# Block attention and expert mixture: first two chunks in plain float32, first block's loads in halves

## The chip, the cores and the metric

One core of a Trainium2 chip. The metric is the device time of one execution in microseconds; lower is better.

## The reference, cut to what matters

q, k, v are 4 × 8 × 576 × 64 float32. Attention is causal by blocks of 64 tokens; its output, laid out as x [2304, 512], goes into a mixture of four experts.

```python
scores = scale * np.matmul(q, k.transpose(0, 1, 3, 2))
mask = (pos[:, None] // 64) >= (pos[None, :] // 64)
attn = softmax(np.where(mask, scores, -1e9))
x = np.matmul(attn, v)                      # as [2304, 512]
p = domain_probs / (domain_probs.sum(-1, keepdims=True) + 1e-9)
for e in range(4):
    h = np.maximum(x @ w1[e], 0.0)          # 512 -> 1024
    out += p[:, e:e + 1] * (h @ w2[e])      # 1024 -> 512
```

## The kernel before, in words

The tokens are cut into a first block of 256 (the first 64 of each of the four batches) and four blocks of 512. The mixture runs through 160 chunks: block by block, expert by expert, eight slices of 128 hidden columns each. A chunk has a first product (`mm1`, L961), a relu and a second product (`mm2`, L1006), which adds into the accumulators of the block's 128-token tiles (two tiles for the first block, four for the others).

Matrix products keep float32 accuracy in split form: an operand is cast to the narrower fp32r type (the high part: xh, w1h, w2h, hh) and the rest is subtracted out (the low part: xl, w1l, w2l, hl), and a product is the sum of three fp32r matmuls. So the first product of a chunk is 12 matmuls (4 slices of the 512 inputs, 3 terms) and the second 3 for each tile. Weights are cast on ACT or DVE (L326, `a_copy`) and subtracted on DVE (L333, `tt`) in `w_split`; the relu is an ACT operation into hh (L978) and a DVE operation into hl (L980).

The attention of the first block (`first_block`, L787 to 903) has no mask and runs in four steps, each for two batches and half of the head pairs: transposes of k and q on PE (L821), copies, scores (L841), then max, subtraction, exp, sum, reciprocal and product (L856 to L866, DVE but for the exp on ACT), transposes (L870), probabilities times V (L883), and the split of the result into xh (ACT) and xl (DVE). PE fills its gaps until the first `mm1` with matmuls on a constant (L345, `warm_up`, 512 columns); WARM = 9 of them stand at the start.

The attention of the other blocks runs in units (one batch, two heads) beside the mixture. A unit transposes k and q on DVE (kT L398, qT L432), has its scores on PE (L510 for the first units, in plain float32), their evacuation on ACT and DVE (tiles S and cm), a column maximum over all partitions on POOL (L644, `m_thread`), a subtraction on DVE, exp on ACT (L660, 128 × 1536 each), and probabilities times V on PE (L723).

The order is made when the kernel is built. Every sequence of operations is a generator; class `Flow` keeps a clock for each engine, and `run` always issues the operation that can start first by its estimate of costs, and among those that can start by then the one with the lowest priority number. It also emits the fill matmuls, as many as its estimate of PE's gap holds. So a changed cost or priority moves instructions on every engine, and what is written behind a waiting instruction on the same engine waits as well. Nearly all loads go out on the SP queue (`dma`, L320); the first block's q and half of its v go out on ACT's. Chunk weights are loaded by `w_thread` (256 KB for each of w1 and w2 of a chunk) into two raw buffers each.

## Time and profile before

| what | value |
|---|---|
| median of 3 runs (lowest, highest) | 935.22 us (934.63, 935.36) |
| profiled execution | 934.92 us |
| its span, instructions | 933.1 us, 12703 |
| PE busy | 922.1 us, 99% of the span |
| weight loads of PE (beside matmuls) | 759.0 us |
| DVE, ACT, POOL busy | 727.8, 424.2, 140.6 us |
| granted clock of PE | 0.999 of full |
| moved by DMA | 107.83 MB, mean 116 GB/s |

The profile is one execution. Busy time of an engine is the union of its instructions; a timeline row gives the start and the duration of one instruction or of several like ones, and in brackets how long the engine stood idle before it and what released it. Matmuls are pipelined: the distance between two starts, not the duration, is what one costs. A matmul in plain float32 leaves two records.

### The profile page before, as it was taken

The numbers are of one execution on the slowest core, as the hardware profiler recorded it, in microseconds if no ns is written. First come the engines' busy times: TensorE is split into PE (matmuls) and PEld (weight loads), VectorE is DVE, ScalarE is ACT, GpSimd is POOL, SyncE is SP. The second block draws the span as 40 slices with busy tenths as digits, with TensorE's granted clock in tenths as the row PEclk, the third lists the DMA queues.
The fourth block names the chain that finished last, engine by engine and source line by source line (L and its number), as shares of the span: only waits on it lengthen the run. The fifth ranks groups of instructions, "written<-read, shape, count | busy, mean of one in ns | idle before, by whom it ended". The sixth has DMA issues, their size and how long they took to land.

```text
span 933.1 us, 12703 instructions
## 1 busy us (share of the span) xinstructions
PE 922.1 (99%) x4381; PEld 759.0 (81%) x4382; DVE 727.8 (78%) x1323; ACT 424.2 (45%) x726; POOL 140.6 (15%) x59
## 2 busy tenths in 40 slices
PE   8999999999999999999999999999999999999998
PEld 4777787888888888888888888888888888888886
DVE  6888879788998988878998889898987754545442
ACT  3477656645565445436454545454434322222220
POOL 2101100131212121212122202112121200000000
PEclk9999999999999999999999999999999999999999
DMA  9765447625352355452523546343523343333311
GB/s 167 169 172 149 125 144 177 160 69 138 89 133 77 102 131 152 97 128 79 142 69 99 127 125 161 100 107 113 116 84 88 99 148 98 95 101 92 100 57 45
DMA packets 235648, 107.83 MB, mean 116 GB/s; under 512 B 130880, under 2 KB 212800, under 8 KB 235584
## 3 DMA queue, kind: packets, MB, share of 16 engines
q1 hardware_dynamic: 232416, 106.24, 43.0%
q10 hardware_dynamic: 3168, 0.79, 0.5%
q8 instruction: 34, 0.56, 0.3%
q14 instruction: 30, 0.25, 0.1%
HBM read 102.27 MB, written 4.72 MB: 115 GB/s over the span
## 4 chain that ended last, share of the span: by engine, by line
PE 94%; DVE 2%; DMA 2%; ACT 1%; SPq 1%; issue 1%; DVEq 0%; ACTq 0%
PE h L961 42%; PE acc L1006 41%; PE att L723 5%; PE att L523 2%; PE att L522 2%; PE acc L723 1%; SPq L320 1%; DMA S<-in_k_dram 0%; DMA w2r<-in_moe_w_dram 0%; PE att L510 0%; DVE cm L333 0%; DMA kr<-in_k_dram 0%; DMA w1r<-in_moe_w_dram 0%; DVE o L1035 0%; PE acc L510 0%
## 5 line engine op out<-in xcount | busy, mean ns | idle before, releaser
L961 PE MATMUL h<-xh,w1h 128*128 128x512 f32 (+1 forms) x640 | 239.1, 374 | 0.6 <-ACT w1h L326 0.6
L961 PE MATMUL h<-xh,w1l 128*128 128x512 f32 (+1 forms) x640 | 236.1, 369 | 1.4 <-DVE w1l L333 1.4
L961 PE MATMUL h<-xl,w1h 128*128 128x512 f32 (+1 forms) x640 | 235.7, 368 | 0.0
L1006 PE MATMUL acc<-w2h,hh 128*128 128x512 f32 x576 | 226.3, 393 | 0.0
L1006 PE MATMUL acc<-w2l,hh 128*128 128x512 f32 x576 | 224.8, 390 | 0.0
L1006 PE MATMUL acc<-w2h,hl 128*128 128x512 f32 x576 | 224.5, 390 | 0.0
L978 ACT ACTIVATE hh<-h 128x512 fp32r<-128x512 f32 (+1 forms) x160 | 88.9, 556 | 206.9 <-PE h L961 204.1
L326 ACT CAST w2h<-w2r 128x512 fp32r<-128x512 f32 x153 | 95.1, 621 | 151.7 <-PE acc L1006 149.1
L333 DVE TENSOR_TENSOR w2l<-w2r,w2h 128x512 fp32r<-128x512 f32 x160 | 109.8, 686 | 53.3 <-ACT w2h L326 52.9
L961 PEld LDWEIGHTS h<-xh,w1h 128*128 128x128 f32 x640 | 120.7, 189 | 22.9 <-issue 2.2
L961 PEld LDWEIGHTS h<-xh,w1l 128*128 128x128 f32 x640 | 120.5, 188 | 22.3 <-DVE w1l L333 2.0
L961 PEld LDWEIGHTS h<-xl,w1h 128*128 128x128 f32 x640 | 120.7, 189 | 19.5 <-DVE xl L333 0.2
L980 DVE SCALAR_TENSOR_TENSOR hl<-h,hh 128x512 fp32r<-128x512 f32 (+1 forms) x160 | 100.8, 630 | 36.4 <-ACT hh L978 35.4
L1006 PEld LDWEIGHTS acc<-w2h,hl 128*128 128x128 f32 x576 | 108.2, 188 | 22.9
L1006 PEld LDWEIGHTS acc<-w2h,hh 128*128 128x128 f32 x576 | 108.3, 188 | 21.2 <-ACT w2h L326 0.7
L1006 PEld LDWEIGHTS acc<-w2l,hh 128*128 128x128 f32 x576 | 108.4, 188 | 20.1
L333 DVE TENSOR_TENSOR w1l<-w1r,w1h 128x512 fp32r<-128x512 f32 x160 | 114.4, 715 | 9.6 <-ACT w1h L326 5.9
L680 POOL PARTITION_ALL_REDUCE S<-S x24 | 81.3, 3437 | 240.2 <-DVE S L333 174.0
L644 POOL PARTITION_ALL_REDUCE mx<-cm x16 | 54.5, 3407 | 358.5 <-DVE cm L333 279.3
L326 ACT CAST w1h<-w1r 128x512 fp32r<-128x512 f32 x115 | 71.2, 619 | 16.7 <-DMA w1r<-in_moe_w_dram 16.4
L326 ACT COPY S<-att 128x512 f32<-128x512 f32 (+2 forms) x88 | 47.5, 540 | 54.5 <-DVE att L589 31.9
L333 DVE TENSOR_TENSOR S<-S,mx 128x1024 f32<-128x1024 f32 (+4 forms) x80 | 60.3, 791 | 4.0 <-POOL mx L644 4.0
(130 smaller groups left out, 855.5 us busy)
## 6 DMA issues: line engine op xcount, KB each, us to landing
w1r<-in_moe_w_dram SPq DMA_DIRECT2D x160, 256.0 KB, 2.9
w2r<-in_moe_w_dram SPq DMA_DIRECT2D x160, 256.0 KB, 2.8
qr<-in_q_dram SPq DMA_DIRECT2D x112, 64.0 KB, 2.3
kr<-in_k_dram SPq DMA_DIRECT2D x64, 72.0 KB, 2.9
out_dram<-o SPq DMA_DIRECT2D x16, 256.0 KB, 2.4
vr<-in_v_dram SPq DMA_DIRECT2D x24, 128.0 KB, 2.6
VN<-in_v_dram SPq DMA_DIRECT2D x8, 128.0 KB, 2.8
S<-in_k_dram SPq DMA_DIRECT2D x4, 128.0 KB, 4.6
```

The source lines that it names most:

```text
L320: o = op(q, 550.0, lambda e: (nc.sync if e == "sp" else nc.scalar).dma_start(out=dst, in_=src), r, u, prio)
L326: o = op(engs, 0, lambda e: nc.scalar.copy(dst, src) if e == "act" else nc.vector.tensor_copy(dst, src), r, u, prio)
L333: o = op(engs, 0, lambda e: ENG[e].tensor_tensor(out=dst, in0=a, in1=b, op=alu), r, u, prio)
L522: nc.tensor.matmul(out=o, lhsT=KK.tile[:, at:at + n], rhs=Hv[:, hs, lo:W], start=True, stop=False)
L523: nc.tensor.matmul(out=o, lhsT=KK.tile[:, at:at + n], rhs=Lv[:, hs, lo:W], start=False, stop=True)
L644: lambda _: nc.gpsimd.partition_all_reduce(mx.tile[:, :2 * W], src, P, RED.max),
L680: st["sums"].append((yield op("pool", 150 + 6.3 * W, lambda _, h=h: nc.gpsimd.partition_all_reduce(Sv[:, h, W:2 * W], Sv[:, h, :W], P, RED ...
L723: nc.tensor.matmul(out=o, lhsT=lhsT, rhs=rhs, start=(i == 0), stop=(i == n - 1))
L961: nc.tensor.matmul(out=ps[:, :n], lhsT=s.tile[:, ks], rhs=x.tile[:, kc, :n], start=(kc == 0 and m == 0), stop=(kc == KC - 1 and m == 2),)
L978: a = yield op("act", 0.833 * n + 55, lambda _: nc.scalar.activation(hh.tile[:, :n], ps[:, :n], AF.Relu), [mm], [pb, hh], 0.0)
L980: l = yield op("dve", 1.04 * n + 70, lambda _: nc.vector.scalar_tensor_tensor(out=hl.tile[:, :n], in0=ps[:, :n], scalar=0.0, in1=hh.tile[: ...
L1006: nc.tensor.matmul(out=acc, lhsT=s.tile[:, ts], rhs=w.tile, start=(f == 0 and m == 0), stop=(f == FC - 1 and m == 2))
```

## The change

- The first block's k and q loads are cut: the first step's halves of k and q go first (k on SP, q on ACT), the other halves of batches 0 and 1 later, on SP (`ORDER`). Chunk 0's w1 is issued on SP, too.
- Chunks 0 and 1 (`WHOLE = 2`) use x, w1, h and w2 as they are, in plain float32 matmuls (`whole1`: four of 256 columns; `whole2`: one of 512 for each tile). There are no splits of their weights, and their relu is one ACT operation (`relu0`). Their weights lie in buffers of the attention that are not used yet. x of the first block is kept whole (x0), and its split into xh and xl is made from that copy by `parts`.
- The costs of the first block's chain are changed by `near` (a lag of −180 ns, 80 ns more for each operation off PE); fill matmuls have 256 columns instead of 512 (the nine first ones keep 512), with a new formula for their number; casts of the weights of chunks 2 to 4 get a lag of 1000 ns; the units' maximum on POOL waits until the mixture is behind chunk 2.

What the order of SP's queue becomes at the start. Before (S1 are k and v of the first block, w1r0 and w2r0 the raw weights of chunk 0, kr, qr, VN the units' k, q and v):

```order
L320 DMA S1_112<-in_k_dram 64x8x64 x4
L320 DMA S1_112<-in_v_dram 64x8x64 x2
L320 DMA w1r0_77<-in_moe_w1_dram 128x4x128
L320 DMA w2r0_79<-in_moe_w2_dram 128x512
L320 DMA kr0_93<-in_k_dram 32x18x32 x4
L320 DMA qr0_95<-in_q_dram 32x16x32 x4
L320 DMA VN0_107<-in_v_dram 64x64
L320 DMA VN0_107<-in_v_dram 128x4x64
```

Now (vr0 is chunk 0's w1, tr0 its w2, qr0 and qT0 with in_moe are chunk 1's weights, w1r and w2r those of chunks 2 and 3):

```order
L342 DMA vr0_96<-in_moe_w1_dram 128x4x128
L342 DMA S1_112<-in_k_dram 64x4x64 x2
L342 DMA S1_112<-in_k_dram 64x8x64 x2
L342 DMA S1_112<-in_v_dram 64x8x64
L342 DMA S1_112<-in_k_dram 64x4x64 x2
L342 DMA cm0_117<-in_q_dram 64x4x64 x2
L342 DMA S1_112<-in_v_dram 64x8x64 x2
L342 DMA tr0_109<-in_moe_w2_dram 128x512
L342 DMA kr0_93<-in_k_dram 32x18x32 x4
L342 DMA qr0_95<-in_q_dram 32x16x32 x4
L342 DMA VN0_107<-in_v_dram 64x64
L342 DMA VN0_107<-in_v_dram 128x4x64
```

Chunk 0's w1 stands ahead of all of k, and its w2 behind k, q and v; the loads of chunks 1 to 3 follow in one row of six behind VN.

SP's queue around the load of chunk 6's w1 (w1r0 in the last row of each piece). Before:

```order
L320 DMA w1r1_78<-in_moe_w1_dram 128x4x128
L320 DMA w2r1_80<-in_moe_w2_dram 128x512
L320 DMA kr1_94<-in_k_dram 32x18x32 x2
L320 DMA qr0_95<-in_q_dram 32x16x32 x4
L320 DMA kr1_94<-in_k_dram 32x18x32 x2
L320 DMA w1r0_77<-in_moe_w1_dram 128x4x128
```

Now:

```order
L342 DMA w2r0_79<-in_moe_w2_dram 128x512
L342 DMA w2r1_80<-in_moe_w2_dram 128x512
L342 DMA kr1_94<-in_k_dram 32x18x32 x2
L342 DMA qr0_95<-in_q_dram 32x16x32 x4
L342 DMA kr1_94<-in_k_dram 32x18x32 x2
L342 DMA probs_n_134<-in_moe_domain_probs_dram 128x4 x4
L342 DMA w1r0_77<-in_moe_w1_dram 128x4x128
```

Four small loads of probs_n that stood ahead of chunk 4's w1 (two rows further up) now stand right ahead of chunk 6's w1. Counted from the start of the queue, 62 loads stood ahead of chunk 6's w1, and now 67.

ACT around the exps of unit 0 (S0, 128x1536). Before (hh1 in the second row shown is chunk 5's relu, w1h2 and w2h2 are chunk 6's casts):

```order
L326 CAST w1h2_63<-w1r0_77 128x512
L978 ACTIVATE hh1_82<-h1_122 128x256
L326 CAST w2h2_71<-w2r0_79 128x512
L660 ACTIVATE S0_111<-S0_111 128x1536
L978 ACTIVATE hh0_81<-h0_121 128x256
L326 CAST w1h3_64<-w1r1_78 128x512
L326 CAST w2h3_72<-w2r1_80 128x512
L660 ACTIVATE S0_111<-S0_111 128x1536
L326 CAST w1h0_61<-w1r0_77 128x512
```

Now (w1h0 and w2h0 are chunk 6's casts, hh1 in the sixth row chunk 5's relu):

```order
L1051 ACTIVATE hh0_81<-h0_121 128x256
L348 CAST w1h0_61<-w1r0_77 128x512
L682 ACTIVATE S0_111<-S0_111 128x1536
L348 CAST w2h0_69<-w2r0_79 128x512
L682 ACTIVATE S0_111<-S0_111 128x1536
L1051 ACTIVATE hh1_82<-h1_122 128x256
L348 CAST w2h1_70<-w2r1_80 128x512
L348 COPY S1_112<-att0_127 128x448
```

Chunk 5's relu stood ahead of both exps and of the cast of chunk 6's w2; now it stands behind them.

The diff, cut to its core:

```diff
-ORDER = [("k", 0), ("q", 0), ("k", 1), ("q", 1), ("v", 0), ("v", 1)]
+ORDER = [("k", 0, 0, 2, "ss"), ("q", 0, 0, 2, "aa"), ("k", 1, 0, 4, "ss"), ("q", 1, 0, 4, "aa"), ("v", 0, 0, 4, "sa"),
+         ("k", 0, 2, 4, "ss"), ("q", 0, 2, 4, "ss"), ("v", 1, 0, 4, "ss")]
 STEPS = [(0, 0, 2), (1, 0, 2), (0, 2, 4), (1, 2, 4)]
+WHOLE = 2
...
             if eng == "pe" and self.fill:
-                n = int(self.FILL * (t - self.clock["pe"]) / 216.0)
+                gap = t - self.clock["pe"]
+                n = int(self.FILL * (gap + 180.0) / 110.0) if gap > 0.0 else 0
...
+    x0 = fl.free["mx"][0].tile.rearrange("p (c w) -> p c w", c=KC)
+    h0s = [fl.free["rc"][0].tile[:, 256 * i:256 * i + 256] for i in range(WHOLE)]
+    wraw = [(fl.free["vr"][0].tile.rearrange("p t h d -> p (t h d)"), fl.free["tr"][0].tile),
+            (fl.free["qr"][0].tile[:, MAXW:], fl.free["qT"][0].tile[:, MAXW:])]
...
+    def near(o):
+        if isinstance(o.eng, list):
+            o.eng = [(e, c + 80.0) for e, c in o.eng]
+        elif o.eng != "pe":
+            o.cost += 80.0
+        o.lag = -180.0
+        return o
...
-            yield ("until", lambda: "S ready" in st)
+            yield ("until", lambda: "S ready" in st and now[0] > WHOLE)
...
+            for name, g, c0, c1, qs in ORDER:
+                if (name, g) not in boxes:
+                    boxes[name, g] = yield fl.take(f"n{name}{g}")
+                bx = boxes[name, g]
+                qs = [{"s": "sp", "a": "act"}[x] for x in qs]
                 if name != "v":
-                    src = {"k": k, "q": q}[name][2 * g:2 * g + 2, :, :MASK_BLOCK, :]
+                    src = {"k": k, "q": q}[name][2 * g:2 * g + 2, 2 * c0:2 * c1, :MASK_BLOCK, :]
                     vals = []
                     for i in range(2):
-                        vals.append((yield dma(bx.tile[64 * i:64 * i + 64].rearrange("p (h d) -> p h d", d=D),
-                                               src[i].rearrange("h r d -> r h d"), MASK_BLOCK * H * D * 4, u=[bx], prio=1.1,
-                                               q="act" if name == "q" else "sp")))
+                        vals.append((yield dma(bx.tile[64 * i:64 * i + 64, c0 * P:c1 * P].rearrange("p (h d) -> p h d", d=D),
...
+            dst = (slice(None), slice(c0, c1), slice(g * P, g * P + P))
+            a = yield near(a_copy(x0[dst], pb.tile[:, :Wc].rearrange("p (c w) -> p c w", w=P), Wc, [t], [pb], pr, True))
+            fl.give(pb)
+            for c in range(c0, c1):
+                xwhole.setdefault(c, []).append(a)
+            fl.spawn(parts(dst, a, Wc, c0, c1))
...
+        def parts(dst, v0, n, c0, c1):
             yield from x_take(0)
             xhb, xlb = X[0]
-            o3 = pb.tile[:, :Wc].rearrange("p (c w) -> p c w", w=P)
-            dst = (slice(None), slice(c0, c1), slice(g * P, g * P + P))
-            a = yield a_copy(xhb.tile[dst], o3, Wc, [t], [pb, xhb], pr, True)
-            l = yield tt("dve", xlb.tile[dst], o3, xhb.tile[dst], SUB, Wc, [t, a], [pb, xhb, xlb], pr)
-            fl.give(pb)
+            a = yield a_copy(xhb.tile[dst], x0[dst], n, [v0], [xhb], 1.3)
+            l = yield tt("dve", xlb.tile[dst], x0[dst], xhb.tile[dst], SUB, n, [a], [xhb, xlb], 1.3)
...
+    def whole_weights():
+        for i, (_, e, f) in enumerate(chunks[:WHOLE]):
+            t1, t2 = wraw[i]
+            v1 = yield dma(t1.rearrange("p (c f) -> p c f", f=P), w1[e, :, f * P:(f + 1) * P].rearrange("(c p) f -> p c f", p=P),
+                           P * DM * 4, prio=w_prio(i))
+            v2 = yield dma(t2, w2[e, f * P:(f + 1) * P, :], P * DM * 4, prio=w_prio(i))
+            wt[i] = (t1, v1, t2, v2)
...
+        yield ("until", lambda: WHOLE - 1 in wt)
+        for i, (_, e, f) in list(enumerate(chunks))[WHOLE:]:
...
+        a = yield late(a_copy(hi.tile, src, DM, [v0], [raw, hi], pr), LATE_W if i < WHOLE + 3 else 0.0)
...
+        if i < WHOLE:
+            yield from whole1(i, n)
+            return
...
+    def whole1(i, n):
+        yield ("until", lambda: i in wt)
+        t1, v1, _, _ = wt[i]
+        pb = yield fl.take("h")
+        ps = pb.tile
+        for kc in range(KC):
+            yield ("until", lambda: len(xwhole.get(kc, ())) == xparts[0])
+            def fn(_, kc=kc):
+                nc.tensor.matmul(out=ps[:, :n], lhsT=t1[:, kc * P:(kc + 1) * P], rhs=x0[:, kc, :n], start=(kc == 0), stop=(kc == KC - 1))
+            if kc == KC - 1:
+                fl.fill = None
+            mm = yield op("pe", 2 * (2 * n / 2.4 + 2.5), fn, [v1] + xwhole[kc], [pb], 3.0)
+        hts[i] = None
+        def relu0():
+            hts[i] = yield op("act", 0.833 * n + 55, lambda _: nc.scalar.activation(h0s[i], ps[:, :n], AF.Relu), [mm], [pb], 0.0)
+            fl.give(pb)
+        fl.spawn(relu0())
...
+    def whole2(i, t):
+        _, _, t2, v2 = wt[i]
+        acc = accs[t].tile
+        def fn(_):
+            nc.tensor.matmul(out=acc, lhsT=h0s[i][:, t * P:(t + 1) * P], rhs=t2, start=(i == 0), stop=False)
+        return op("pe", 2 * (2 * DM / 2.4 + 2.5), fn, [hts[i], v2], [], 3.0)
```

## Rows read from the trace of the kernel before

**Rows 1.** Busy time by stretches (start:end, length, each engine's busy us and instructions, clock):

```profile
80.00:900.00 820.00, 818.55 (x3826) 681.63 (x3825) 655.67 (x1154) 376.89 (x628) 129.13 (x38) 1.00 0.42 114
...
sum 933.10, PE 922.11 PEld 758.96 DVE 727.85 ACT 424.20 POOL 140.58; mean PE 115.26 PEld 94.87 DVE 90.98 ACT 53.02 POOL 17.57
```

**Rows 2.** What PE waited for over the span (us in total, times, longest):

```profile
PE h L961 <- DVE w1l L333: 1.4, 2, 1.1
```

**Rows 3.** Timeline of DVE in the opening (start, duration, operation, idle before and releaser):

```profile
10.59 0.42 DVE L856 TENSOR_REDUCE st<-acc 128x4 f32<-128x256 f32 x1 [1.95 <-PE acc L841]
...
15.30 0.42 DVE L326 CAST w1h<-w1r 128x512 fp32r<-128x512 f32 x1
...
16.03 0.68 DVE L333 TENSOR_TENSOR w1l<-w1r,w1h 128x512 fp32r<-128x512 f32 x1
...
24.88 0.77 DVE L398 STREAM_TRANSPOSE kT<-kr 128x576 f32<-128x576 f32 x1
```

**Rows 4.** Timeline of PE, 26 to 54 us:

```profile
26.52 0.69 PE L510 MATMUL acc<-qT,kT 64*128 64x512 f32 x1
...
28.33 0.39 PE L961 MATMUL h<-xh,w1h 128*128 128x256 f32 x1
...
29.24 0.53 PE L510 MATMUL acc<-qT,kT 64*128 64x320 f32 x1
...
30.30 0.50 PE L1006 MATMUL acc<-w2h,hh 128*128 128x512 f32 x1
...
32.48 0.33 PE L510 MATMUL att<-qT,kT 64*64 64x64 f32 x4 [1.20 <-DVE cm L333]
...
33.55 0.28 PE L961 MATMUL h<-xh,w1h 128*128 128x256 f32 x1
...
34.96 0.40 PE L1006 MATMUL acc<-w2h,hh 128*128 128x512 f32 x1
...
36.35 0.28 PE L961 MATMUL h<-xh,w1h 128*128 128x256 f32 x1
...
46.61 0.39 PE L1006 MATMUL acc<-w2h,hl 128*128 128x512 f32 x1
47.26 0.39 PE L961 MATMUL h<-xh,w1h 128*128 128x256 f32 x1 [0.26 <-ACT w1h L326]
...
49.28 0.40 PE L1006 MATMUL acc<-w2h,hh 128*128 128x512 f32 x1
...
50.67 2.81 PE L723 MATMUL acc<-S,VN 128*128 128x512 f32 x10
53.41 0.53 PE L510 MATMUL acc<-qT,kT 64*128 64x320 f32 x1
```

**Rows 5.** Timeline of ACT, 46 to 51 us:

```profile
46.59 0.62 ACT L326 CAST w1h<-w1r 128x512 fp32r<-128x512 f32 x1 [3.37 <-DMA w1r<-in_moe_w_dram]
47.11 0.38 ACT L978 ACTIVATE hh<-h 128x256 fp32r<-128x256 f32 x1
48.48 0.62 ACT L326 CAST w2h<-w2r 128x512 fp32r<-128x512 f32 x1 [0.99 <-DMA w2r<-in_moe_w_dram]
49.00 1.48 ACT L660 ACTIVATE S<-S 128x1536 f32<-128x1536 f32 x1
50.39 0.36 ACT L978 ACTIVATE hh<-h 128x256 fp32r<-128x256 f32 x1
```

**Rows 6.** Timeline of the SP queue, its issues (start, time to issue all of them):

```profile
32.97 1.92 SPq L320 DMA_DIRECT2D probs_n<-in_moe_domain_probs_dram  x4
...
38.04 4.30 SPq L320 DMA_DIRECT2D qr<-in_q_dram  x4
...
43.54 0.42 SPq L320 DMA_DIRECT2D w1r<-in_moe_w_dram  x1
```

**Rows 7.** Loads, 0 to 50 us (KB each, median us from issue to landing):

```profile
S<-in_k_dram SPq DMA_DIRECT2D x4, 128.0 KB, 4.6
...
probs_n<-in_moe_domain_probs_dram SPq DMA_DIRECT2D x4, 1.0 KB, 2.5
```

More of the change, by code (lines that the diff above doesn't have):

```diff
@@ L342, with warm_up @@
     ones, spare = nc.const_aps.tensor(1.0, [P, 512], mybir.dt.bfloat16), fl.free["h"][1].tile
-    def warm_up():
-        nc.tensor.matmul(out=spare, lhsT=ones[:, :P], rhs=ones, start=True, stop=True)
+    def warm_up(n=256):
+        nc.tensor.matmul(out=spare[:, :n], lhsT=ones[:, :P], rhs=ones[:, :n], start=True, stop=True)
     def identity():
@@ L815, in step @@
             for x in "kq":
[L816 to L817 removed]
+                yield ("until", lambda: (x, g, c0) in raw)
+                bx, vals = raw[x, g, c0]
                 T_ = yield fl.take("f" + x)
@@ L869, in step @@
             for c in range(m):
[L870 to L871 removed]
+                tp = yield near(op("pe", 200.0, lambda _, o=pb.tile[:, c * P:(c + 1) * P], i_=S_.tile[:, c * P:(c + 1) * P]: nc.tensor.transpose(
+                    o, i_, ident), [t], [pb, S_], pr))
             fl.give(S_)
             PT = yield fl.take("fp")
[L874 removed]
+            a = yield near(a_copy(PT.tile[:, :Wc], pb.tile[:, :Wc], Wc, [tp], [pb, PT], pr, True))
             fl.give(pb)
[L876 to L877 removed]
+            yield ("until", lambda: ("v", g, c0) in raw)
+            VD, vv = raw["v", g, c0]
             pb = yield fl.take("att", None, ("early", "early2"))
@@ L925, in w_split @@
     def w_split(which, i, raw, src, v0, pr):
-        hi = yield fl.take(f"w{which}h", i)
-        lo = yield fl.take(f"w{which}l", i)
-        a = yield a_copy(hi.tile, src, DM, [v0], [raw, hi], pr)
+        hi = yield fl.take(f"w{which}h", i - WHOLE)
+        lo = yield fl.take(f"w{which}l", i - WHOLE)
+        a = yield late(a_copy(hi.tile, src, DM, [v0], [raw, hi], pr), LATE_W if i < WHOLE + 3 else 0.0)
         o = tt(BOTH, lo.tile, src, hi.tile, SUB, DM, [a], [raw, hi, lo], pr)
@@ L990, in mm2 @@
         n = sizes[bi]
+        if i < WHOLE:
+            yield ("until", lambda: hts[i] is not None and i in wt)
+            if i == 0:
+                yield ("until", lambda: len(fl.free["early"]) == 2)
+            for t in range(n // P):
+                o = whole2(i, t)
+                if i == 0:
+                    o.r = o.r + [Val(accs[t].last)]
+                yield o
+            return
         yield ("until", lambda: hts[i] is not None and (i, 2) in wt)
@@ L998, in mm2 @@
                 deps.append(free_acc[t])
-                if i == 0 or (e == 0 and bi == 1):
-                    yield ("until", lambda: len(fl.free["early2" if bi else "early"]) == 2)
+                if e == 0 and bi == 1:
+                    yield ("until", lambda: len(fl.free["early2"]) == 2)
                     deps.append(Val(accs[t].last))
```

69 lines of the change are left out of this document (32 added, 37 removed).

## The prediction

> **What bounds the kernel now.** First the page's busy times and the table by stretches: TensorE (PE) is busy 922.1 us, and from 80 to 900 us it stands still for 1.45 of 820 us [rows 1]. There every microsecond is a matmul; the change removes none there, so it can pay only in the opening, where PE waits, and can cost there or wherever it makes PE wait anew. Then the list of what PE waited for: the longest wait for a weight split is 1.1 us [rows 2]. Then the timelines of the opening, where PE's longest wait stands, 1.20 us of L510 for a VectorE (DVE) operation on cm [rows 4]. On DVE the first block's softmax chain runs from 10.6 us almost without a gap until kT, the transpose for attention unit 0, at 24.88; among the chain stand splits of weights, w1h 0.42, w1l 0.68 and w2l as long as w1l, and the same three a second time [rows 3]. On PE unit 0's scores begin at 26.52, chunk 2's first matmul at 33.55, chunk 3's at 36.35, chunk 6's at 47.26, chunk 5's second product at 49.28, unit 0's probabilities times V at 50.67 [rows 4]. On ScalarE (ACT), the cast of chunk 6's w1 waits 3.37 us for its load and starts at 46.59; chunk 5's relu stands right behind it, at 47.11, and so waited as well [rows 5]. SP, the queue of nearly all loads, issues that load at 43.54 [rows 6].
>
> **The change, part by part, from the profiled execution (934.92 us; the median of the runs is 0.30 above).**
>
> *Loads in halves.* A K half is now two issues of 64 KB, but chunk 0's w1 of 256 KB goes ahead of it on SP. The first K tile took 4.6 us from issue to landing in the median of four [rows 7]. Ahead of the first K half's end now stand 256 + 128 KB where the whole tile was 256. I give the halving no gain for the first pair. Later pairs and the 256-column fill matmuls may gain some tenths (the chain's first reduce waited 1.95 us for PE, to 10.59 [rows 3]); that stands in a bound below.
>
> *Splits out of the first block's DVE chain.* Two times 0.42 + 0.68 + 0.68 = 3.56 us of DVE work go [rows 3], about 0.3 less for overlap; two casts of x into xh come to DVE, at no more than the 0.42 of a cast twice as wide, and one of four xl subtractions of about 0.4 moves behind kT. That is 3.56 − 0.3 − 0.8 + 0.4 = 2.9 us less ahead of kT. I take 2.3, since kT now stands behind a cast that needs ACT's copy of x first, where DVE will wait some. Bounds: 3.3 if the loads and fills give 0.4 too; 1.0 if the chain, with DVE lighter, waits for ACT and PE instead. **Unit 0's scores start at 24.2 instead of 26.52: −2.3.**
>
> *Plain float32.* Unit 0's first five plain products (512 + 448 + 320 + 192 + 64 = 1536 columns, two records each) run from 50.67 to 53.41 [rows 4], 1.78 ns a column: 0.457 us for 256 columns, 0.913 for 512. The split form takes 1.41 us for twelve at 256 columns (33.55 to 34.96) and 1.39 for six at 512 (34.96 to 36.35) [rows 4]. Two chunks: 8 × 0.457 + 4 × 0.913 = 7.3 against 5.6, so +1.7; three of the first four 256-column products lie in PE's idle time inside the first block. What is left stands in the next step.
>
> *From unit 0's scores to chunk 3.* Before, 26.52 to 33.55 is 7.03. In the new order the same stretch holds unit 0's scores (1.81, 1.06 and 0.33 [rows 4]), five whole-float products of 256 (2.29), two of 512 (1.83): 7.3. It no longer has the wait of 1.20 [rows 4], since the copy to cm that L510 waited for stood behind a split of w1 on DVE, and in the new order the splits there belong to chunks 2 and 3, whose loads should have landed. Against that chunk 0's relu on ACT stands behind two casts that wait for the last of six weight loads in a row: I put 0.2 there (0 to 1.5). So 7.5 for 7.03, +0.5. Chunk 1's second product: 1.83 for 1.39, +0.4. **At chunk 3 PE is 1.4 us ahead** (0 to 2.5).
>
> *What takes the lead.* Chunk 6's w1 decides next. Before, PE had done with chunk 4's second product by about 46.9, and waited for it [rows 4]. SP had 62 issues ahead of that load and now has 67; at the pace of the four of probs_n, 1.92 us [rows 6], five more are 2.4. The four qr issues that took 4.30 [rows 6], 2.4 over that pace, may shrink by as much. I take the landing where it was, 46.6 (44.4 to 47.5). **Lead gone: +1.4** (0 to 2.5).
>
> *A new wait on ACT.* Behind the cast of chunk 6's w1, ACT's order is now exp, cast of w2, exp, and only then chunk 5's relu; before, the relu stood ahead of both. With a cast's step 0.52 (46.59 to 47.11) and an exp's 1.39 (49.00 to 50.39) [rows 5]: 46.59, exp 47.11, w2 48.50 (its load is there by 48.48), exp 49.02, relu 50.41, done at about 50.8. PE wants it for chunk 5's second product, at 49.28 before [rows 4]. **+1.5** (0 to 1.6; it vanishes only with an earlier landing). Unit 0's second head has its exp sooner, but PE gets there after both anyway.
>
> *Afterwards.* PE arrives about 1.5 us later at all that follows, in an order of DVE and ACT that was planned for an earlier PE. No row shows these waits. All idle time of PE from 80 to 900 us is 1.45 [rows 1], the longest wait for a split 1.1 [rows 2]. I add 0.7 (0 to 1.9). The all-reduce on POOL, now held until chunk 2 is done in the planner's count, lies beside PE: 0.
>
> Sum: −2.3 + 0.5 + 0.4 + 1.4 + 1.5 + 0.7 = +2.2 on 934.92, so 937.1, and 937.4 in terms of the median.
>
> The trace doesn't show how the loads of SP and ACT share the engines. The Trainium skill ("DMA: Bandwidth & Descriptors", Queues, rings and completion order) says that each DMA engine takes turns between the rows of the issuing queues, packet by packet, with one row for SP and one for ACT; by that rule q on ACT overtakes chunk 0's w1 and K on SP doesn't, so the halved q buys nothing, and the first pair starts by its K. No run here shows it yet; it speaks against this change, and rival three below is that mechanism, priced from rows.
>
> **The rivals.**
>
> *One: the lead lives.* If the qr issues no longer stall (2.4 us) and the added issues fall in SP's pauses, chunk 6's w1 lands by the lead earlier, 45.2, and the whole ACT sequence with it. For: the stall of 4.30 is there to win. Against: five more issues, and all of them ahead. Sum: −1.4 + 1.5 + 0.7 = +0.8, so 936.0 in terms of the median: no change.
>
> *Two: faster.* The DVE gain at its upper end, and nothing of it given back: −3.3 + 0.5 + 0.4 = −2.4, so 932.8 in terms of the median. It decides at chunk 5's relu: PE then wants it at 46.9, and the sequence from landing to relu takes 4.2 us, so chunk 6's w1 must land before 42.7. For: the DVE chain is nearly solid, so that removed work should shorten it. Against: the load has to come 3.9 us sooner from a queue that has more to issue.
>
> *Three: halves do not do what they say.* K's first half lands later than the whole did, behind 256 KB: K's first tile took two loads of 128 KB and 4.6 us, where a load of 1 KB takes 2.5 [rows 7], so 2.1 for 256 KB and 1.05 for the 128 KB more. Then the chain, SP's later issues and chunk 6's load all come 1 us later: the lead is only 0.4, but it was to be lost anyway, and the landing at 47.6 adds 1.0: +3.2, so 938.4.
>
> **How the numbers follow.** A measurement of this kernel tells 0.2% (1.9 us) from no change: the border lies at 937.1 above and 933.4 below. Forecast 0.48, of which 0.35 lie over the border (the terms of 1.5 and 0.7 can shrink); rival one 0.24, all but 0.03 within; rival two 0.12; rival three 0.16, slower. So faster 0.13, same 0.34, slower 0.53: 0.35 + 0.16 + 0.02 slower, 0.11 + 0.02 faster. The forecast's own range is 935.5 to 939.3 (with 1.9 for afterwards and 0.2 more at the relu). The range takes in rival one and most of three, and leaves out rival two and what is beyond either bound: 934.0 to 939.4.
>
> **What would show it.** Right, step by step: unit 0's scores at about 24.2; whole-float products at 0.46 and 0.91 us; chunk 3's first matmul 0.8 to 2.5 us before 36.35; chunk 6's first at 47 with a wait for the cast of its w1; right after it, PE's longest wait, about 1.5 us, for chunk 5's relu, with two exps ahead of that relu on ACT; probabilities times V near 52.2. Wrong: chunk 6's load landing before 45, so that chunk 5's relu is ready in time; or scores of unit 0 no earlier than 26, which would throw the DVE step; or a granted clock below full between 20 and 30 us, where 256-column fills replace longer ones.

## The result, and the profile after

| what | before | after |
|---|---|---|
| median (lowest, highest) | 935.22 us (934.63, 935.75) | 943.22 us (941.93, 944.98), 5 runs |
| ratio after / before, 95% interval | | 1.0087 (1.0073 to 1.0101) |
| profiled execution, its span | 934.92, 933.1 us | 943.41, 941.6 us |
| PE busy | 922.1 us | 927.5 us |
| DVE, ACT busy | 727.8, 424.2 us | 723.2, 429.9 us |

Slower by 8.0 us, where 2.2 were forecast, and outside the range. What PE of the changed kernel waited for over the span (us in total, times, longest):

```profile
PE h L1004 <- ACT w1h L348: 3.6, 2, 2.5
PE acc L1089 <- ACT hh L1051: 2.2, 2, 1.4
PE att L544 <- DVE cm L355: 1.5, 2, 1.1
```

Two stretches of its table of busy times, PE alone (start:end, length, PE busy and instructions, clock, DMA share, GB/s):

```profile
155.00:160.00 5.00, 4.03 (x16) 0.67 0.70 228
...
80.00:900.00 820.00, 815.18 (x3806) 1.00 0.42 114
```

Between 80 and 900 us PE stands still for 4.8 us, against 1.45 before [rows 1], and over the whole span the two waits for ACT's casts of w1 alone cost 3.6 us, 1.1 at 49 us and 2.5 at 155. From 155 to 160 us the granted clock is 0.67: part of that stretch ran at the lower of TensorE's two levels, 1.2 GHz. Before, the clock was full through that edge.

The opening in the timeline of DVE (first reduce, kT):

```profile
8.33 0.42 DVE L882 TENSOR_REDUCE st<-acc 128x4 f32<-128x256 f32 x1 [1.11 <-PE acc L867]
...
21.60 0.77 DVE L420 STREAM_TRANSPOSE kT<-kr 128x576 f32<-128x576 f32 x1
```

And in that of PE (first scores of the block, unit 0's scores, chunk 1's second product, chunk 3's second matmul):

```profile
7.62 0.66 PE L867 MATMUL acc<-o,o 128*64 128x128 f32 x8
...
23.59 1.13 PE L532 MATMUL att<-qT,kT 64*128 64x512 f32 x4
...
33.00 1.88 PE L1043 MATMUL acc<-qT,rc 128*128 128x512 f32 x4
...
34.84 0.28 PE L1004 MATMUL h<-xl,w1h 128*128 128x256 f32 x1
```

The first reduce is 2.3 us earlier than in [rows 3], kT 3.3, unit 0's scores 2.9 [rows 4]. Chunk 1's second product is four records from 33.00 on. Chunk 3's second matmul is at 34.84, and its first lies one step of 0.12 ahead of it, so the product takes 1.72 us, 0.86 for 512 columns. Before, chunk 3's second matmul was one step of 0.12 behind the first at 36.35 [rows 4]: PE is 1.6 us ahead there. So far the sum is as forecast or better. Then the loss begins. PE from 42 to 55 us, from its wait for chunk 3's relu on:

```profile
42.80 0.50 PE L1089 MATMUL acc<-w2h,hh 128*128 128x512 f32 x1 [0.80 <-ACT hh L1051]
...
48.14 0.39 PE L1089 MATMUL acc<-w2h,hl 128*128 128x512 f32 x1
49.63 0.38 PE L1004 MATMUL h<-xh,w1h 128*128 128x256 f32 x1 [1.10 <-ACT w1h L348]
...
50.35 0.38 PE L1004 MATMUL h<-xh,w1l 128*128 128x256 f32 x1 [0.23 <-DVE w1l L355]
...
53.18 0.50 PE L1089 MATMUL acc<-w2h,hh 128*128 128x512 f32 x1 [1.38 <-ACT hh L1051]
...
55.00 0.67 PE L745 MATMUL att<-S,VN 128*128 128x512 f32 x1 [0.15 <-issue]
```

The last matmul of chunk 4's second product is at 48.14, where it was at 46.61 before [rows 4]. So PE is 1.5 us behind even before it waits for chunk 6: the lead is gone, and 3.2 us are lost between chunk 3 and here. Of these, 0.8 is the wait at 42.80. Another 0.9 is in unit 1's first scores, which take 2.69 us (35.87 to 38.56) where they took 1.81 (37.87 to 39.68); in the timeline of the kernel before, the products of the unit's two heads start in pairs at the same time, and here the second pair does not. Some 0.4 is in small parts. The last 1.1 is only moved: unit 1's scores of 320 and 192 columns now stand here, at 45.47, and no longer behind unit 0's product with V, at 53.41 [rows 4]. Even without it PE is 0.4 behind.

PE at the block's edge:

```profile
155.13 0.39 PE L1004 MATMUL h<-xh,w1h 128*128 128x256 f32 x1 [2.48 <-ACT w1h L348]
...
156.47 0.38 PE L1004 MATMUL h<-xh,w1l 128*128 128x256 f32 x1 [0.84 <-DVE w1l L355]
...
156.87 0.41 PE L1004 MATMUL h<-xl,w1h 128*128 128x256 f32 x1
157.08 0.41 PE L1004 MATMUL h<-xh,w1l 128*128 128x256 f32 x1
```

ACT in these places:

```profile
40.00 1.38 ACT L348 CAST w2h<-w2r 128x512 fp32r<-128x512 f32 x2 [2.93 <-DMA w2r<-in_moe_w_dram]
...
42.34 0.41 ACT L1051 ACTIVATE hh<-h 128x256 fp32r<-128x256 f32 x1
...
48.96 0.62 ACT L348 CAST w1h<-w1r 128x512 fp32r<-128x512 f32 x1 [5.82 <-DMA w1r<-in_moe_w_dram]
49.48 1.48 ACT L682 ACTIVATE S<-S 128x1536 f32<-128x1536 f32 x1
50.87 0.60 ACT L348 CAST w2h<-w2r 128x512 fp32r<-128x512 f32 x1
51.38 1.48 ACT L682 ACTIVATE S<-S 128x1536 f32<-128x1536 f32 x1
52.77 0.36 ACT L1051 ACTIVATE hh<-h 128x256 fp32r<-128x256 f32 x1
...
153.00 0.62 ACT L348 CAST VS<-vr 128x512 fp32r<-128x512 f32 x1 [1.25 <-DMA vr<-in_v_dram]
153.52 1.04 ACT L348 CAST HH<-qT 128x1024 fp32r<-128x1024 f32 x1
154.47 0.61 ACT L348 CAST w1h<-w1r 128x512 fp32r<-128x512 f32 x1
```

Chunk 3's relu, at 42.34, stands behind two casts of w2 (chunks 4 and 5) that waited 2.93 us for their loads, and behind copies of unit 1's scores. Chunk 6's w1 is cast at 48.96, not 46.6 [rows 5]; behind it come exp, cast of w2, exp, and chunk 5's relu at 52.77, for which PE waits 1.38 us. At the edge PE waits 2.48 us for the cast of chunk 31's w1, which stands behind unit 4's VS and HH, then 0.84 for its split; from 156.87 matmuls of 256 columns start 0.21 us apart instead of 0.12. The timeline of SP's queue (start, time to issue all of them) tells why the loads of chunks 6 and 31 were late:

```profile
20.78 4.25 SPq L342 DMA_DIRECT2D kr<-in_k_dram  x4
25.07 3.15 SPq L342 DMA_DIRECT2D VN<-in_v_dram  x4
...
39.28 2.60 SPq L342 DMA_DIRECT2D qr<-in_q_dram  x4
...
43.42 1.92 SPq L342 DMA_DIRECT2D probs_n<-in_moe_domain_probs_dram  x4
45.86 0.38 SPq L342 DMA_DIRECT2D w1r<-in_moe_w_dram  x1
...
143.54 6.00 SPq L342 DMA_DIRECT2D qr<-in_q_dram  x8
...
150.72 0.44 SPq L342 DMA_DIRECT2D w1r<-in_moe_w_dram  x1
```

Chunk 6's w1 is issued at 45.86, before 43.54 [rows 6]. All issues ahead of it take 41.75 us together where they took 39.40. The five added ones are 2.1 of that, all q loads give 1.6 back (the last four 1.7: 2.60 for 4.30), and the VN loads take 1.5 more; four of these (3.15), and the four of kr (4.25), stand behind six weight loads in a row (17.63 to 20.74). The loads of probs_n ahead of it are eight in both kernels and cost the same. At the edge eight q loads of unit 4 take 6.00 us and stand ahead of chunk 31's weights; in the kernel before they took 4.22 and stood one chunk later, ahead of chunk 32's, and the waits there are the 1.45 us of [rows 1].

PE's lead over the kernel before, by the first matmul of a chunk: 1.6 us ahead at chunk 3, 2.4 behind at chunk 6, 3.2 behind at chunk 30, 6.9 behind at chunk 33, 8.7 behind from chunk 128 on. The 3.7 at the edge are waits (3.32 for 1.45) and half of some 3.4 us at the lower clock (1.7); behind the edge two waits for cm (1.5). Comparisons at one chunk carry some tenths of attention work that the new order has moved.

### The profile page after: what moved, and what is told of

Its sections match the earlier page's. It is cut to its first block, busy times and chain, and to the rows that moved or that the text cites. A ratio compares the mean times of both kernels' runs of the same rounds, so it can differ in the third digit from the quotient of the medians.

```text
span 941.6 us, 12739 instructions
## 1 busy us (share of the span) xinstructions
PE 927.5 (99%) x4411; PEld 763.5 (81%) x4411; DVE 723.2 (77%) x1307; ACT 429.9 (46%) x736; POOL 139.7 (15%) x59
## 4 chain that ended last, share of the span: by engine, by line
PE 92%; DVE 4%; DMA 2%; SPq 1%; ACT 1%; issue 1%; ACTq 0%; DVEq 0%
PE acc L1089 39%; PE h L1004 39%; PE att L745 5%; PE att L545 2%; PE att L544 2%; PE acc L745 1%; SPq L342 1%; PE h L367 1%; DVE w2l L355 1%; DVE w1l L355 1%; DMA w1r<-in_moe_w_dram 1%; DVE o L1118 0%; PE acc L532 0%; PE att L532 0%; DVE S L355 0%
## 5 line engine op out<-in xcount | busy, mean ns | idle before, releaser
L348 ACT CAST w2h<-w2r 128x512 fp32r<-128x512 f32 x150 | 93.2, 622 | 142.9 <-PE acc L1089 139.1
L348 ACT COPY S<-att 128x512 f32<-128x512 f32 (+2 forms) x93 | 49.4, 533 | 65.5 <-DVE att L611 38.4
```

The lines of the kernel that those rows point to most:

```text
L348: o = op(engs, 0, lambda e: nc.scalar.copy(dst, src) if e == "act" else nc.vector.tensor_copy(dst, src), r, u, prio)
```

## The experiments

Some kernels below keep the changed kernel's order and move single operations behind another one, by a table in which each entry names an operation and the one that it now follows (("load", 2, 7) is the load of chunk 7's w2, ("probs", 1) the loads of probs_n for block 1, ("qr", 4, ..), ("VS", 4) and the like belong to unit 4); the others change a constant or undo a part. Each was timed beside the kernel before, whose median lay between 934.46 and 935.25.

### One wait at a time

```diff
+HOLD = {("probs", 1): ("load", 2, 7)}                                              # e_probs
+HOLD = {("qr", 4, 1, j): ("load", 2, 31), ("vr", 4): ("load", 2, 31),              # e_edge, j = 0 to 3
+        ("VS", 4): ("split", 2, 31), ("HH", 4): ("split", 2, 31)}
+HOLD = {("exp", 0, 0): ("relu", 5), ("cast", 2, 6): ("relu", 5), ("exp", 0, 1): ("relu", 5)}   # e_relu, e_relu2
```

e_all and e_all2 hold all three.

e_probs:

> The changed kernel with four small loads (probs_n of the second block) put behind chunk 7's weights on SP instead of ahead of chunk 6's. Theory (SP's count of issues sets when chunk 6's w1 lands): issue at 43.9 instead of 45.86, landing at 47.0 instead of 48.96, PE's wait of 1.10 before chunk 6 goes, the relu wait stays near 1.3, the time falls by 1.5 to 2.0 us. Rival (the load waits for its buffer or for the DMA engines, not for SP): landing within 0.5 of 48.96, time the same within 0.5.

e_edge:

> The changed kernel with the loads of chunk 31's weights ahead of half of unit 4's q and of its v on SP, and its casts and splits ahead of unit 4's on ACT and DVE. Theory (PE's 2.48 and 0.84 us before chunk 31 come from a load and a cast that stand behind unit 4's, and the half clock of 3.4 us right after comes from that idle stretch): the waits shrink to under 0.6 together, PE's granted clock stays full from 150 to 165 us, and the time falls by 4 to 5 us. Rival one (the clock falls for another reason): clock still at half for 3.4 us near 157, time down by 2.5 to 3. Rival two (unit 4 becomes late instead): a wait of 2 to 3 us of unit 4's scores at about 157, time down by under 1.5.

e_relu:

> The changed kernel, with its planned order kept but for one place: on ACT, chunk 5's relu is issued ahead of unit 0's first exp, chunk 6's w2 cast and the second exp. Theory (a wait in the opening is paid to the end): PE's wait of 1.38 us for that relu at 53.18 goes, unit 0's product with V starts some 1.5 earlier, and the time falls by 1.3 to 1.6 us. Rival (the loads set the pace, and the wait moves to the next load or to the end of the first block): the time falls by under 0.5.

e_all:

> The three moves together (relu ahead of the exps; probs_n behind chunk 7's weights; chunk 31's weights ahead of unit 4's second half). Theory: 7 to 8.5 us less than the changed kernel, so 934.7 to 936.2, since the three waits are in series on PE; then plain float32 and halves themselves cost nothing here. Rival (the waits hide one another, or the plain chunks cost by themselves): 938 or more.

e_relu2:

> As e_relu, but chunk 8's load of w2, which takes the buffer of chunk 6's, is also kept behind the moved cast (in e_relu it was issued ahead of it, so that ACT waited for that load and chunk 6 used chunk 8's w2). Theory: PE's wait for chunk 5's relu goes; 1.3 to 1.6 us less than the changed kernel. Rival (waits only move): under 0.5 less.

e_all2:

> The three moves together with that load kept behind. Theory: the waits before chunk 6, for chunk 5's relu and before chunk 31 are in series, and the half clock of 3.4 us at 157 goes with the last: 6 to 8 us less than the changed kernel, 935 to 937. Rival: what is won before chunk 6 is lost at the split of its w1 or of its low part, as with probs_n moved alone, and only the stretch at 150 us is won: 3 to 4.5 us less, 939 to 940.

| kernel | median us | ratio (interval) |
|---|---|---|
| e_probs | 942.81 | 1.0079 (1.0062 to 1.0096) |
| e_edge | 944.12 | 1.0089 (1.0067 to 1.0111) |
| e_relu | 947.97 | 1.0136 (1.0119 to 1.0154) |
| e_all | 949.27 | 1.0148 (1.0129 to 1.0166) |
| e_relu2 | 943.55 | 1.0086 (1.0070 to 1.0103) |
| e_all2 | 945.67 | 1.0115 (1.0099 to 1.0132) |

None differs from the changed kernel's 1.0087 (1.0073 to 1.0101) to the better by more than the intervals; e_all2 is if anything worse. In e_relu and e_all the load of chunk 8's w2 came into the buffer ahead of the moved cast, so chunk 6 was multiplied with chunk 8's w2 and waited for it: they compute something else and tell nothing of the relu. In the others the waits moved on or others came. The timelines of e_probs, of DVE:

```profile
49.78 0.17 DVE L1153 TENSOR_REDUCE probs_s<-probs_n 128x4 f32<-128x16 f32 x1 [3.07 <-DMA probs_n<-in_moe_domain_probs_dram]
49.88 0.69 DVE L372 TENSOR_TENSOR w1l<-w1r,w1h 128x512 fp32r<-128x512 f32 x1
```

of PE:

```profile
50.63 0.39 PE L1021 MATMUL h<-xh,w1l 128*128 128x256 f32 x1 [1.97 <-DVE w1l L372]
...
53.58 0.50 PE L1106 MATMUL acc<-w2h,hl 128*128 128x512 f32 x1 [1.03 <-DVE hl L1070]
```

Chunk 6's w1 was issued at 43.11 and cast at 46.40, so its landing follows SP's queue, and that part of the theory holds. Even so PE reached chunk 6 only at 48.27, since the lead had been lost ahead of it. Then the reduce over the moved probs loads stood ahead of the split of chunk 6's w1 on DVE and waited for them: 1.97 us where 1.10 + 0.23 had been. The wait for the relu became one for hl, 1.03 (the last row). e_relu2 shows the same for hl (1.16) with the relu in time: hl stands behind the split of w2 on DVE. e_edge's two waits at the edge went from 2.48 and 0.84 to 1.32 and 1.01, and its profile, the fastest of its four executions (941.26), has the full clock there; but the clock was at the lower level for 6.8 us from 39.4 on, behind stops of 1.16 and 0.56. e_all2 waits 1.60 and 1.01 at the edge, and its clock falls there, at 155.8, for 6.8 us.

### Each half of the change alone

f_whole has the two plain chunks with what goes with them (chunk 0's w1 ahead of k, the lag of the casts, POOL's gate) and the first block's loads, costs and fills as before; f_halves has the halves, `near` and the 256-column fills, with WHOLE = 0 and no load of w1 ahead of k.

```diff
-ORDER = [("k", 0, 0, 2, "ss"), ("q", 0, 0, 2, "aa"), ("k", 1, 0, 4, "ss"), ("q", 1, 0, 4, "aa"), ("v", 0, 0, 4, "sa"),
-         ("k", 0, 2, 4, "ss"), ("q", 0, 2, 4, "ss"), ("v", 1, 0, 4, "ss")]
+ORDER = [("k", 0, 0, 4, "ss"), ("q", 0, 0, 4, "aa"), ("k", 1, 0, 4, "ss"), ("q", 1, 0, 4, "aa"), ("v", 0, 0, 4, "sa"),
+         ("v", 1, 0, 4, "sa")]                                        # f_whole, and near, fills, chain costs as before
-WHOLE = 2
+WHOLE = 0                                                             # f_halves
```

f_whole:

> Plain float32 in chunks 0 and 1 alone, with its lags and the gate on POOL: the first block's loads whole, its planned costs and the fill matmuls (512 columns) as before. Theory (new waits behind late loads, from SP's and ACT's planned order): ACT again has unit 0's exps ahead of chunk 5's relu, and SP eight issues of q, k and probs_n ahead of chunk 6's w1, so 940 to 945. Rival one (it is the halves and the chain's costs): within 2 of before. Rival two (any new plan costs so much): 940 to 945 here and in the halves alone too.

f_halves:

> The halves, the chain's costs and lags and the 256-column fill matmuls alone: chunks 0 and 1 in split form, no load of w1 ahead of k. Theory (the loss comes with the plain chunks' order of loads and relus): within 2 us of before, 933 to 937, with the first block ended 0.5 to 1.5 us earlier. Rival (the loss comes with the halves): 939 or more.

f_whole took 939.97 (1.0054, 1.0039 to 1.0069), f_halves 940.97 (1.0063, 1.0048 to 1.0078). DVE's first reduce and kT in f_whole:

```profile
10.38 0.42 DVE L876 TENSOR_REDUCE st<-acc 128x4 f32<-128x256 f32 x1 [1.11 <-PE acc L861]
...
22.06 0.77 DVE L414 STREAM_TRANSPOSE kT<-kr 128x576 f32<-128x576 f32 x1
```

The same two in f_halves:

```profile
6.56 0.42 DVE L882 TENSOR_REDUCE st<-acc 128x4 f32<-128x256 f32 x1 [0.84 <-PE acc L867]
...
25.47 0.77 DVE L420 STREAM_TRANSPOSE kT<-kr 128x576 f32<-128x576 f32 x1
```

The splits alone bring kT 2.8 us earlier [rows 3], with the first reduce where it was. The halves alone bring the first reduce 4.0 us earlier and kT later by 0.6: the chain gives the head start back before its end. Both halves alone are slower than the kernel before, so f_halves' rival came, not its theory. f_whole's time lies just below its theory's range, but its profile doesn't show the reason given: its long wait is one of 4.25 for qT. Each has a stretch of lower clock (f_whole at 40 us, behind that wait; f_halves a second one at 154). In f_halves PE stood 2.76 us from 22.85 on; its row of PE's timeline:

```profile
25.61 0.58 PE L1006 MATMUL h<-xl,w1h 128*128 128x256 f32 x1 [2.76 <-DVE xl L355]
```

and the stretch behind it, 24.7 to 31.5 us, in the table of busy times, with the clock at 0.51 (it began at 24.5, inside the stop):

```profile
24.70:31.50 6.80, 5.89 (x19) 0.51 0.79 198
```

### The same costs in another order

One constant of the order's estimate, 300 to 305 ns or 120 to 125 ns, re-plans most of the program without changing its work.

```diff
-    LAT = 300.0
+    LAT = 305.0          # n1: kernel before, a1: changed kernel
-    SELF = 120.0
+    SELF = 125.0         # n2: kernel before, a2: changed kernel
```

n1:

> The kernel before, with one constant of its planner (the latency between engines) at 305 ns instead of 300: the work is the same, only the planned order differs (on some 1,000 lines). Theory (the order of loads and of ACT's operations, not the added work, sets these microseconds): such a plan differs from before by more than 1 us in either direction. Rival (the plan hardly matters; the plain chunks and halves cost by themselves): within 1 us of before, 934 to 936.2.

n2:

> The same with another constant (an engine's wait for its own result) at 125 ns instead of 120. Theory: more than 1 us from before in one direction or the other. Rival: within 1 us.

a1:

> The changed kernel, all of it, with the latency constant at 305 instead of 300. Theory (its loss is that of one plan): a time that differs from 943.2 by more than 2 us, most likely lower, since a plan with three such waits is a bad one. Rival (the loss belongs to plain chunks and halves in any order): 941.5 to 945.

a2:

> The changed kernel, all of it, with the constant for an engine's own result at 125 instead of 120. Theory: differs from 943.2 by more than 2 us, most likely lower. Rival: 941.5 to 945.

| order | kernel before | changed kernel | difference |
|---|---|---|---|
| as shipped | 935.22 | 943.22 | 8.0 |
| LAT 305 | 937.80, 1.0033 (1.0023 to 1.0043) | 941.73, 1.0064 (1.0047 to 1.0081) | 3.9 |
| SELF 125 | 936.45, 1.0015 (1.0006 to 1.0024) | 940.59, 1.0057 (1.0038 to 1.0077) | 4.1 |

Ratios are against the kernel before as shipped. Re-planned, that kernel gets slower both times, by more than the 1 us of n1's and n2's theory: its order as shipped is the fastest of the three. The changed one comes out lower both times, by 1.5 us (inside a1's rival) and by 2.6 (a2's theory), though its intervals still overlap with 1.0073 to 1.0101. The kernel before has no stretch of lower clock inside its profile; all four of these have one, a1 and a2 near the edge (at 158.6 and 153.7), n2 behind a wait of 2.42 for cm, and n1 behind this wait of PE:

```profile
33.18 0.33 PE L510 MATMUL att<-qT,kT 64*64 64x64 f32 x4 [2.01 <-DVE cm L333]
```

(its table of busy times, PE alone, 33 to 38 us: clock 0.66)

```profile
33.00:38.00 5.00, 4.82 (x23) 0.66 0.56 104
```

Two orders each are a small sample, and each difference is uncertain by some 2 us; by this estimate about half of the 8.0 us belongs to the order and not to the work.

### The clock at the edge, and the waits taken together

c_fill keeps order and waits and gives PE something to do in the edge's stop; nothing reads these products.

```diff
+STOP_GAP = {31: 14}
...
+                for _ in range(STOP_GAP.get(i, 0) if kc == 0 else 0):
+                    nc.tensor.matmul(out=ps, lhsT=ones[:, :P], rhs=ones, start=True, stop=True)
...
+HOLD = {("exp", 0, 0): ("hl", 5), ("cast", 2, 6): ("hl", 5), ("exp", 0, 1): ("hl", 5),      # g_two
+        ("probs", 1): ("load", 2, 7), ("sum", 1): ("split", 2, 7)}
+HOLD = {("cast", 1, 6): ("exp", 0, 0), ("exp", 0, 1): ("hl", 5), ("cast", 2, 6): ("exp", 0, 1),   # h_two
+        ("cast", 2, 7): ("exp", 0, 1), ("probs", 1): ("load", 2, 7), ("sum", 1): ("split", 2, 7)}
```

g_fill is g_two with STOP_GAP = {31: 14}; g_all is g_two and h_all is h_two, each with e_edge's moves and STOP_GAP = {31: 6}.

c_fill:

> The changed kernel, and ahead of chunk 31's first product 14 products of the constant ones, 512 columns each, into that chunk's own bank (nothing reads them): PE works through the stop of 2.48 us instead of standing. The waits themselves stay as they were. Theory (PE's standing is what is followed by the half clock at 156.7): the stretch of 3.41 us is gone, 1.7 us less: 941.5; with the fills' overrun of up to 0.5 us, 941.5 to 942. Rival (the half clock comes from something else in the block's change, the fp32r products with their three terms or a fixed place in the run): the stretch stays near 156, 943.2 or slightly more. Second rival: the stretch moves to a later wait, same time.

g_two:

> The changed kernel with the waits of 45 to 53 us taken away together, as they stand in series on the queues: chunk 5's relu and its split hl ahead of unit 0's exps on ACT and DVE, and the four loads of block 1's domain values with the reduce that waits for them behind chunk 7's weights on SP and DVE. All else in its order. Theory (the waits are in series, and each alone only hands its time to the next): chunk 6's w1 is issued 1.9 us earlier, the waits 1.10, 0.23 and 1.38 shrink to under 1 us together, products after chunk 6 begin 1.5 to 2 us earlier than in the changed kernel; 941.0 if the edge at 152 and its half clock stay. Rival (a further queue takes the wait up): drift at chunk 28 stays at +3, 943.

g_fill:

> The two edits before this one together (waits of 45 to 53 us, and the 14 products ahead of chunk 31). Theory: their gains add, as one is PE's waiting and the other its clock: 3 to 3.5 us under the changed kernel, 939.5 to 940. Rival: as the products now come earlier, they wait longer for the edge's weights, and the gain of the first is lost there: 941.5.

g_all:

> The waits of 45 to 53 us, the edge's loads and casts (chunk 31's weights ahead of half of unit 4's queries and of its values on SP, its casts and splits ahead of unit 4's on ACT and DVE) and 6 products of the constants ahead of chunk 31. Theory: of the drift of 8.5 us against the kernel before, some 2 us of block 0, 1 us of the edge and 1.7 us of the half clock go: 938 to 939, still above the kernel before, whose own plan has fewer stops. Rival: the half clock comes elsewhere instead, at one of the stops that are left, and the time stays at 941 or above.

h_two:

> The changed kernel with unit 0's first exp ahead of chunk 6's w1 cast on ACT (ACT stands idle 5.82 us there with the exp's scores ready at 46.5), chunk 5's relu next, then the second exp and only then the casts of w2; block 1's domain values behind chunk 7's weights as in the run before. In that run the exps stood behind a weight cast and the PV product waited 2.14 us for them. Theory (block 0's loss is ACT's queue, in which the exps stand behind loads): second exp done by 51.5, PV product without a wait, the waits of 45 to 55 us under 1 us together, drift at chunk 28 from +3.2 to about +1.2. Whether the time follows depends on the edge: if its wait is set by the load queue, it grows from 2.9 to some 5 us and the time stays at 943 to 944; if it is set by what PE released earlier, 941 to 942. Rival: another queue takes it up again in block 0 and chunk 28 stays at +3.

h_all:

> The same, with the edge's loads, casts and splits moved as before and 6 products of the constants ahead of chunk 31. Theory (waits in series, all taken together): drift at chunk 28 about +1.2, edge waits 1.3 and 1.0, clock full: 939 to 940. Rival: edge waits grow by what block 0 gave back, 941 to 942.5 as the run without the exps' move.

| kernel | median us | ratio (interval) | first matmul of chunk 30 against before | lower clock at (us) |
|---|---|---|---|---|
| c_fill | 941.40 | 1.0069 (1.0056 to 1.0082) | +3.1 | none |
| g_two | 944.00 | 1.0094 (1.0081 to 1.0108) | +3.3 | 157 |
| g_fill | 941.46 | 1.0069 (1.0056 to 1.0082) | +5.4 | 56 |
| g_all | 942.43 | 1.0078 (1.0065 to 1.0091) | +3.5 | none |
| h_two | 943.20 | 1.0083 (1.0070 to 1.0096) | +3.5 | 30, 156 |
| h_all | 941.38 | 1.0075 (1.0063 to 1.0088) | +1.9 | 156 |

The last two columns are of the profiled executions; the stretch at the very end, behind the last products, is in all and left out. PE of c_fill at the edge:

```profile
152.63 3.01 PE L1006 MATMUL h<-const-bfloat16-1.0 128*128 128x512 bf16 x13
155.62 0.39 PE L1008 MATMUL h<-xh,w1h 128*128 128x256 f32 x1
...
156.96 0.39 PE L1008 MATMUL h<-xh,w1l 128*128 128x256 f32 x1 [0.84 <-DVE w1l L357]
157.18 0.28 PE L1008 MATMUL h<-xh,w1h 128*128 128x256 f32 x1
157.30 0.29 PE L1008 MATMUL h<-xl,w1h 128*128 128x256 f32 x1
```

and the table of busy times there, clock 1.00 where the changed kernel had 0.67:

```profile
155.00:160.00 5.00, 4.16 (x23) 1.00 0.68 214
```

The fills stand from 152.63 to 155.62 (13 of the 14 are recorded), the wait of 0.84 behind them is as before, and the clock stays full: 0.12 us from matmul to matmul. The median is 1.8 us lower, about half of 3.4 us, as c_fill's theory had it. The two intervals still overlap, but the mean granted clock of all five executions is 0.999 to 1.000, against 0.996 to 0.998 in the changed kernel's five. (In this execution the wait of 1.10 at 48 us is missing too, as PE came to it later; at chunk 30 it stood as the changed kernel did.) So it was the stop of 2.48 us that brought the clock down, and not the products or the place in the run. The Trainium skill ("TensorE: Matmul & The Clock Gate", Part 1) says that PE's own busy-ness gates its clock; this run agrees.

g_two takes the waits of 48 to 53 us out of the profile, 1.10 + 0.23 + 1.38, and the product of probabilities and V waits 2.14 instead. (Its table also put chunk 7's w2 cast ahead of the exps, which its expectation doesn't say.) So g_two's rival came, another queue. g_fill had its edge filled and met the lower clock behind that other stop, at 56 us; its 941.46 is its rival's time, not the 939.5 to 940 of two gains that add. h_two has the second exp on ACT done at 51.73, and the product still waits 1.27. PE:

```profile
55.32 1.10 PE L765 MATMUL att<-S,VN 128*128 128x512 f32 x2 [1.27 <-issue]
```

DVE in the same place (reduce, operation on cm):

```profile
53.89 0.17 DVE L1156 TENSOR_REDUCE probs_s<-probs_n 128x4 f32<-128x16 f32 x1
...
54.60 0.62 DVE L375 TENSOR_TENSOR cm<-att,S 128x448 f32<-128x448 f32 x1
```

The product writes the bank that unit 1's scores lay in, and the last reader of that bank is the operation on cm at 54.60, done at 55.22. In the three profiles of the changed kernel, g_two and h_two that operation ends at 54.90, 55.06 and 55.22, and the product starts 0.10 later each time (55.00, 55.16, 55.32). The moved reduce, with its three small operations, now stands ahead of it. So h_two's theory, that all hangs on the exps' place on ACT, fell: the operation on cm holds the product, and DVE's queue holds that operation, with two splits of w2 and the four operations on probs ahead of it, while the copy from ACT that it needs is done at 53.18. No run moved these operations alone. Of h_two's drift 1.7 us are a lower clock at 30 us, which the changed kernel's profile doesn't have.

h_all has its theory's signs in part: +1.9 at chunk 30, but waits of 0.97 and 1.01 at the edge, and the lower clock behind them; its time, 941.38, lies in its rival's range. g_all stood 1.24 and 1.01 there, and its clock stayed full; its 942.43 is its rival's time. No version is faster than the kernel before; with intervals this wide the order among c_fill, g_fill, g_all and h_all is open.

## Why the prediction was wrong

The sign's likeliest case, slower, came, but 8.0 us and not 2.2; the range ended at 939.4. By its steps:

- *Loads in halves: no gain for the first pair.* Wrong for the pair: its K half landed in 3.5 us (median of two issues) where the whole tile took 4.6 [rows 7], and the block's first scores came 2.3 us earlier, at 7.62. K's own transposes start only 0.2 earlier than before (5.64), q's 1.4 earlier (6.65), so more than K's landing is in the 2.3. Right for the chain's end: f_halves' kT is not earlier. Rival three, K held up by chunk 0's w1, has its mechanism but not its result: in f_halves, with no w1 ahead, the K halves landed in 2.7 us and K's transposes began at 4.30, 1.3 us sooner than in the changed kernel; in f_whole, with w1 ahead of the whole K, they began at 7.60, where the kernel before has 5.88. So w1 does hold K up, and the halving paid for it with 0.2 us left over. By the rule cited for it, turns between queues, the halved q was to buy nothing; no run here takes q and k apart.
- *Splits out of the chain: −2.3.* Right and somewhat small: f_whole's kT has −2.8, the changed kernel −2.9 at unit 0's scores.
- *Plain float32: 0.457 and 0.913.* Right, and close: 0.475 for 256 columns (two between 25.94 and 26.89, with the change to the next product) and 0.86 for 512.
- *Lead at chunk 3: 1.4.* Right in the sum, 1.6, by two errors that offset each other: the splits gave 0.6 more, and the stretch from unit 0's scores to chunk 3 cost 1.3 instead of 0.9. In it unit 0's scores of 320 and 192 columns took 1.54 us (26.89 to 28.43) where they had taken 1.06 [rows 4], with the second head's products starting 0.5 later.
- *Chunk 6's w1 decides next, and lands where it was, 46.6.* This step failed first, and twice. The path was wrong: I had put nothing between chunk 3 and this load, and there PE lost its whole lead and 0.4 us more (0.8 for chunk 3's relu, 0.9 in unit 1's scores, 0.4 in small parts) and took over 1.1 of moved scores. e_probs shows it: with the cast at 46.40 PE came to chunk 6 no sooner than 48.27, where it was 47.26 before. The landing was wrong, too: 48.96. The added issues cost 2.1, near my 2.4, but q gave back only 1.6, and the VN loads took 1.5 more, a term I had not named.
- *Chunk 5's relu behind two exps: +1.5.* Right in place and size, 1.38, from a later landing. But e_relu2 removes this wait, and the time does not fall: a wait of 1.16 for hl shows instead.
- *Afterwards: +0.7.* This step failed most, being mis-sized and without the clock. From chunk 30 on PE loses 5.5 us more: 1.9 of waits at the edge, 1.7 of lower clock, 1.5 at cm. I had taken the bound from PE's idle time of before (1.45), a row of another order; and the order after the change is a new one on every engine, which I knew and priced as if it were the old one a little late. The row that spoke, eight q loads of unit 4 ahead of chunk 31's weights, is in SP's order of the changed kernel; I did not read that far. The clock had no term at all: I named it only for 20 to 30 us, where it stayed full.

What the runs settle: the lower clock at the edge comes from PE's stop (c_fill), and the waits of 48 to 55 us are a series on ACT's and DVE's queues, each of which covers the next (e_probs, e_relu2, g_two, h_two). What they don't: which of the waits a good order would keep, and how much of the 8.0 us between the medians is clock, since other executions of the kernel before have mean clocks of 0.995 to 1.000. About 4 us of the 8 were there in both other orders as well, and the parts that these share were not taken apart: 1.7 for plain float32 by the forecast, the six weight loads in a row, and one part that looks like work. Up to 60 us PE is busy with the units' plain float32 scores for 6.7 us in the kernel before, n1 and n2, and for 7.5 to 8.2 in the changed kernel, a1, a2, f_whole and f_halves, since the two heads' products start together less often. Why they do is open.

## What to carry to other kernels

Where a planner sets the order, a change of costs buys a new order, not the old one with an edit: re-plan the kernel before as well (n1, n2) before a difference of 1% is put down to the change. Read the changed order at every block's edge, not only where the edit is, and price each wait there twice: once as the wait and once as the clock that may fall behind it. Look for losses in busy time as well as in waits: two products that no longer run side by side are counted as work. A wait that is taken out of one in-order queue is worth only what the next queue's wait leaves.
